# A hand-ordered attention and gate kernel: PSUM banks written into a table, and the compute tasks put in another order

## The chip, the cores and the metric

The kernel runs on one core of a Trainium2 chip. The metric is the device time of one execution in microseconds (us), as the median of several runs. PE is the matrix engine, DVE the vector engine, ACT the scalar engine, POOL the general engine, SP the engine that issues most transfers.

## The reference

Attention over 8 batches, 12 heads, 448 positions and 64 numbers a head, in which the sum below the fraction has one more term; then a gate with a circular convolution along the positions, between two dense layers (D is 768):

```python
scores = q @ k.transpose / 8                     # (8, 12, 448, 448)
m = max(scores); e = exp(scores - m)
x = (e / (sum(e) + exp(-m) + 1e-9)) @ v          # then heads side by side: (8, 448, 768)
x1, x2, x3 = split(x @ w_proj)                   # w_proj (768, 2304)
x2_conv = irfft(rfft(x2, axis=1) * rfft(filter, axis=0))
y = x1 * x2_conv * x3
out = y @ w_out                                  # (8, 448, 768), float32
```

Inputs and output are float32 in HBM; the matmuls run in bfloat16.

## The kernel before, in words

**Tasks.** Nothing is issued while the tensors are walked through. Each piece of work (four matmuls, one evacuation of PSUM, one transfer) is added to a plan with `plan.add` (line 83): the engine, what it needs and makes, the buffers that it takes and gives back, and a function that issues it. The plan then hands out the tasks. Each engine issues its tasks in the order of their numbers in `plan.ORDER` (line 455), a tuple with one number for each of 2033 tasks. `plan.FLIP` (line 456) lists the tasks that run on their other engine, ACT instead of DVE or the reverse. An engine works strictly in the order issued: a task that waits holds up all that stand behind it on that engine, and the wait itself is put in from what the task reads and writes.

**PSUM.** There are 8 banks. Scores ("sc", up to 3 at once) and attention outputs ("op", up to 2) take pairs of banks, everything else ("hy", up to 5) one bank. Which bank a task gets is chosen by `spots` (line 171) among those that the plan believes to be free at that moment, mostly the one that has been free longest. A matmul that writes into a bank waits for whatever last read that bank.

**Work.** `attention(i)`, i from 0 to 47, does one pair of heads. On PE: the scores S (lines 947 and 952, four matmuls of 64 rows for each of four tiles), the last 64 keys' part of e times v (ER, line 977), the rest of it (V, line 997). On ACT: the exponentials e and er (line 966). On DVE: the division, `norm` (lines 1010 to 1012, result xb). Results go to the transposed activations xT by a DMA transpose (line 1056). `dense(b)` does one batch of the gate: on DVE the folds that make xf (lines 1125 and 1134); on PE the projection x2, called PS (line 1175); its copy and a DMA transpose that SP issues (line 1188, in two halves); the spectrum Z on PE (line 1223) and its copy xs; the product with the filter's spectrum, t and yh, on DVE (lines 1241 and 1247); the inverse I on PE (line 1319) with its copy cr; cw, cv and the last product y on DVE (lines 1335, 1337, 1346, 1361). The gates G (line 1273) are six matmuls each; x1 is the copied one, and g is x1 times the other, on DVE (line 1288). The output O (line 1091, begun four matmuls early as O4) goes through the copy os into one of three buffers osb and is stored by SP (lines 1403, 1406, 1409). All copies out of PSUM stand in one helper, line 486 on ACT and line 488 on DVE. The buffers osb are taken in turn, so the copy of a fourth output tile waits until the store of the first has landed.

**Order of the whole.** The dense work of batch b runs between the attention tasks of later batches. Loads of q, k, v and their DMA transposes run far ahead on SP's queue; POOL casts what was loaded (lines 733 and 759) and issues v and the weights. At the start PE turns q and k itself for two batches (T, lines 621 to 642; copies qT and kT), the tables of the transform are built (rps at line 847; its copy fr, lines 854 and 855 on ACT), and the filter's spectrum is taken (uw on DVE, hrs). Where the plan expects PE to be idle at the start it puts filler matmuls (line 1566); 38 more (line 1574) run first of all.

Of the kernel before, what the change touches and what calls it, by code (L numbers as in the profile page):

```python
# [41 lines left out]
class Plan:  # L42
# [17 lines left out]
    FLIP = ()  # L60
    FETCH = (4.6, 256, 150)
# [14 lines left out]
    def __init__(self, rings):  # L76
        self.size = rings
        self.tasks = []
        self.banks = {}
        self.kept = []  # L80
        self.open = []

    def add(self, eng, cost, want, emit, need=(), make=(), take=(), give=(), dma=0.0, run=256, n=1, after=0.0, begun=(), late=0.0, turn=False, part=None, keep=False, port=False, mode=None, alt=None, mm=None):
        if alt:
            own = (eng, cost)
            (eng, cost), alt = (alt, own) if len(self.tasks) in self.FLIP else (own, alt)
            emit = lambda f=emit, e=eng: f(e)
        want = self.ORDER[len(self.tasks)] if self.ORDER else want + self.SHIFT.get(part, 0.0)
        self.tasks.append((want, len(self.tasks), eng, cost, emit, need, make, take, give, dma, after, run, n, begun, late, turn, keep, port or eng == "POOL" and not dma, mode or ("full" if eng == "PE" and not keep else None), alt, 2 * (mm or max(1, round(cost / 0.17)) if eng == "PE" and cost else 0)))

    def run(self):
# [79 lines left out]
        def spots(t):  # L171

            found, count = {}, {}
            for r, tok in t[7]:
                if r not in self.CAP or (r, tok) in self.banks:
                    continue
                count[r] = count.get(r, 0) + 1
                have = sum(1 for o in self.banks if o[0] == r and gone.get(o, 1e9) > now + 1e-9)
                if have + count[r] > self.CAP[r]:
                    return None  # L180
                busy = {i for got in found.values() for i in got}
                open_ = [i for i in range(self.NBANKS) if i not in busy and until[i] <= now + 1e-9]
                if r in self.PAIRS:
                    pairs = [(max(until[i], until[i + 1]), i) for i in open_ if i % 2 == 0 and i + 1 in open_]
                    if not pairs:
                        return None
                    i = min(pairs)[1]
                    found[(r, tok)] = (i, i + 1)
                else:
                    if not open_:  # L190
                        return None
                    found[(r, tok)] = (min(open_, key=lambda i: (self.MATE and i ^ 1 in open_, i < self.LOW, until[i], i)),)
            return found

        def ready(t):
            e = t[2]
            if not self.ORDER and t[10] > now + 1e-9:
                return False
            for k in t[5]:
                if made.get(k, 0):  # L200
                    return False
                at, by = when.get(k, (0.0, e))
                if at + (self.LAT[by] if by != e else 0.0) > now + 1e-9:
                    return False
            if e in queues and t[9]:
                out = sum(h[2][12] for h in queues[e]) + sum(x > now + 1e-9 for x in landed[e])
                if out + t[12] > self.OPEN:
                    return False
            if spots(t) is None:
                return False  # L210
            new = {}
            for r, tok in t[7]:
                if (r, tok) in holds or r in self.CAP:
                    continue
                h = held[r]
                i = len(h) + new.get(r, 0) - self.size[r]
                new[r] = new.get(r, 0) + 1
                if i >= 0 and gone.get((r, h[i]), 1e9) > now + 1e-9:
                    return False
            return True  # L220

        while any(queue.values()):
            moved = False
            for e in queue:
# [9 lines left out]
                for key, at in spots(t).items():  # L234
                    self.banks[key] = at
                    for j in at:
                        until[j] = 1e9
# [9 lines left out]
                if t[20]:  # L247
                    after, block, shift = self.FETCH
                    wait, cost = 0.0, end - now
                    edge = (fed - shift) // block * block + block + shift  # L250
                    while edge <= fed + t[20]:
                        at = now + cost * (edge - fed) / t[20] + wait
# [35 lines left out]
        for i, (_, t) in enumerate(order):  # L288
            if i in full:
                self.fill(*full[i])  # L290
            if t[16]:
                mine = {x for key in t[8] for x in self.banks.get(key, ())}
# [46 lines left out]
def kernel(  # L339
# [101 lines left out]
    def couple(c):  # L441
# [6 lines left out]
    plan = Plan(  # L448
        {
            "e": NE, "er": 2 * NER, "k0": 2, "q0": 2, "u": 1, "w": 1, "xf": 1,  # L450
            "x2": 1, "x2s": 1, "x2h": 1, "xs": 2, "t0": 2, "t1": 2, "yh": 1, "g": 1, "x1": 2, "cr": 2, "cw": 1, "cv": 2, "yT": 1, "yR": 1,
            "os": 3,
        }
    )
# [61 lines left out]
    def staged(b):  # L516
# [3 lines left out]
        for hp in range(NHP):  # L520
# [6 lines left out]
            for n, (name, x, at, size) in enumerate(parts):  # L527
# [29 lines left out]
                if alone:  # L557
                    add("ACT" if first else "SP", 0.52 if first else 0.5, -21.0 if first else want + 0.1 * n, load,
                        make=[("s" + name, g)], after=hold, dma=0.95 if name == "q" else 0.71, run=50)
                elif hp % 2 == 0:  # L560
                    need = [("cv", g - 6), ("cv", g - 5)] if name == "v" and c >= 3 else []
                    if name != "v" and c >= 4:
                        need = [("c" + w, c - 4) for w in "kq"]
                    add("POOL", 0.73, want + 0.1 * n, load, need=need, make=[(made, g), (made, g + 1)], after=hold, dma=1.05 if name == "q" else 1.0, run=45)
                if hp == 0 and name != "q":
                    add("SP", 2.6, want + (0.05 if name == "k" else SLOT[0] + 0.05) if b == 0 else want - RE1 + 0.1 * n,
                        lambda name=name: rests_load(name, b),
                        need=[("cr" + name, b - 1)] if b else (), make=[("r" + name, b)],
                        dma=1.25, run=22, begun=[("ir", b)], n=4)
# [1055 lines left out]
    with (  # L1625
# [6 lines left out]
        for b in range(n_batches):  # L1632
            W["yT", b], W["yR", b // 2] = y, yr
            stable(b)
            plan = Plan(plan.size)
# [9 lines left out]
    with tc.manual_schedule(engines={E.PE, E.Pool, E.DVE, E.Activation, E.SP}):  # L1645
        plan = main
# [31 lines left out]
```

## Time and profile before

| What | Value |
|---|---|
| runs | 373.08, 374.23, 373.16 us; median 373.16 |
| profiled execution, span | 370.8 us (the page gives no other time of that execution) |
| PE busy | 356.4 us, 96% |
| DVE busy | 274.8 us, 74% |
| ACT busy | 237.5 us, 64% |
| POOL busy | 127.6 us, 34% |
| clock granted to PE, 40 slices | 9 tenths or more in each |

The span runs from the first to the last recorded work; the runs' times are about 2.4 us longer than it. "Busy" of PE counts overlapping pipelined matmuls, so 96% doesn't mean that only 4% is left to win, nor that so much can be won. A wait shows in the timeline as a bracket at the row that waited, with the engine, the tile and the line that it waited for.

### The profile page before, as it was taken

Reading aid. Unit: us, or ns where it says so; the run is one execution under the profiler, and the core shown is the slowest. Engines: PE = TensorE matmul, PEld = TensorE weight load, DVE = VectorE, ACT = ScalarE, POOL = GpSimd, SP = SyncE. Lnnn points to the kernel's source line nnn. Section 1 sums busy time; section 2 is a strip of 40 time slices with the busy share of each in tenths; the row PEclk is TensorE's granted clock in tenths of the full one; section 3 lists DMA queues with packets and bytes.
Section 4 is the critical chain, followed back from the end, with each engine's and each line's share of the span. In section 5 each row is a group of like instructions: output and inputs, shape, how many; then the busy total and the mean of one; then the engine's idle time right before and its main releaser. Section 6 shows DMA issues by size and latency. Waiting matters only on the chain. (4 is left out here: it accounts for less than half of the span.)

```text
span 370.8 us, 10707 instructions
## 1 busy us (share of the span) xinstructions
PE 356.4 (96%) x4300; PEld 211.8 (57%) x4300; DVE 274.8 (74%) x674; ACT 237.5 (64%) x379; POOL 127.6 (34%) x278
## 2 busy tenths in 40 slices
PE   7989999999999979999999999999999999999995
PEld 7666675554555545565555646665565655555552
DVE  5468659982789726897579977689459898779970
ACT  4999876756767548567565657867776561334343
POOL 9984251444625274265537523313100100000000
PEclk9999999999999999999999999999999999999999
DMA  9999999988999999999998799995830074125035
GB/s 169 194 191 204 207 207 205 206 169 160 168 242 156 229 214 208 235 242 192 206 182 202 166 245 192 262 208 122 171 72 1 7 196 89 42 45 170 4 129 172
DMA packets 133958, 61.93 MB, mean 167 GB/s; under 512 B 105165, under 2 KB 130704, under 8 KB 133904
## 3 DMA queue, kind: packets, MB, share of 16 engines
q1 hardware_dynamic: 111552, 48.71, 61.6%
q0 software_dynamic: 22112, 12.26, 25.4%
q8 instruction: 34, 0.56, 0.6%
q10 hardware_dynamic: 240, 0.23, 0.2%
q14 instruction: 20, 0.16, 0.2%
HBM read 43.86 MB, written 11.01 MB: 148 GB/s over the span
## 5 line engine op out<-in xcount | busy, mean ns | idle before, releaser
L966 ACT ACTIVATE e<-psum 128x896 bf16<-128x896 f32 x144 | 126.6, 920 | 40.8 <-PE psum L947 37.3
L1273 PE MATMUL psum<-xT,wproj_bf 128*128 128x448 bf16 x576 | 121.7, 353 | 0.1
L1273 PEld LDWEIGHTS <-wproj_bf 128*128 128x128 bf16 x576 | 53.4, 98 | 47.7 <-issue 5.0
L1091 PE MATMUL psum<-wout_bf,yT 128*128 128x384 bf16 x288 | 54.7, 326 | 0.8 <-DVE g L1288 0.4
L1175 PE MATMUL psum<-xf,wproj_bf 128*128 128x452 bf16 x252 | 53.9, 357 | 0.0
L947 PE MATMUL psum<-qT,kT 64*64 64x448 bf16 x576 | 45.4, 359 | 2.5 <-DVE g L1288 0.7
L997 PEld LDWEIGHTS <-e 128*128 128x128 bf16 x1152 | 42.0, 98 | 9.6 <-issue 5.2
L997 PE MATMUL psum<-vn,e 128*128 128x65 bf16 x1152 | 46.8, 194 | 0.0
L733 POOL CAST nat<-nat 112x512 bf16<-112x512 f32 x36 | 25.4, 708 | 44.7 <-DMA nat<-in_q_dram 41.8
L1241 DVE TENSOR_TENSOR t<-xs,hrs 113x768 bf16<-113x768 bf16 (+1 forms) x64 | 36.4, 578 | 2.9 <-ACT xs L486 2.3
L1288 DVE TENSOR_TENSOR g<-x,psum 128x448 bf16<-128x448 bf16 x48 | 29.2, 616 | 12.1 <-PE psum L1273 10.9
L1091 PEld LDWEIGHTS <-yT 128*128 128x128 bf16 x288 | 26.6, 98 | 19.9 <-issue 1.8
L1175 PEld LDWEIGHTS <-wproj_bf 128*128 128x128 bf16 x252 | 23.2, 96 | 22.2 <-issue 1.1
L486 ACT CAST x<-psum 128x448 bf16<-128x448 f32 (+1 forms) x39 | 20.4, 529 | 22.6 <-PE psum L1273 14.5
L759 POOL CAST nat<-nat 128x384 bf16<-128x384 f32 x36 | 21.5, 598 | 32.2 <-DMA nat<-in_k_dram 31.9
L486 ACT COPY osb<-psum 128x384 f32<-128x384 f32 x39 | 18.2, 486 | 20.1 <-PE psum L1091 15.9
L486 ACT CAST xs<-psum 113x384 bf16<-113x384 f32 (+1 forms) x41 | 19.2, 482 | 15.1 <-PE psum L1223 14.1
L1012 DVE TENSOR_TENSOR xb<-psum,den 128x896 bf16<-128x896 f32 x24 | 26.2, 1091 | 0.8
L486 ACT CAST cr<-psum 128x452 bf16<-128x452 f32 x35 | 18.0, 539 | 11.5 <-PE psum L1319 11.0
L947 PEld LDWEIGHTS <-kT 64*64 64x64 bf16 x576 | 15.6, 105 | 17.1 <-issue 12.9
L966 ACT ACTIVATE er<-psum 128x896 bf16<-128x896 f32 x24 | 22.2, 926 | 4.3 <-PE psum L952 3.5
L987 POOL MEMSET sinks<- 1x1 bf16 x18 | 1.6, 91 | 65.6 <-PE psum L977 65.6
(143 smaller groups left out, 501.3 us busy)
## 6 DMA issues: line engine op xcount, KB each, us to landing
nat<-in_q_dram SPq DMA_DIRECT2D x37, 224.0 KB, 3.8
out_dram<-osb SPq DMA_DIRECT2D x21, 384.0 KB, 3.5
nat<-in_k_dram SPq DMA_DIRECT2D x38, 192.0 KB, 3.9
nat<-in_v_dram POOLq DMA_DIRECT2D x15, 192.0 KB, 6.3
wproj_bf<-in_moe_w_proj_dram POOLq DMA_DIRECT2D x2, 1152.0 KB, 18.1
out_dram<-osb SPq DMA_DIRECT2D x12, 192.0 KB, 2.7
ks<-in_v_dram POOLq DMA_DIRECT2D x9, 192.0 KB, 4.9
rests<-in_k_dram SPq DMA_DIRECT2D x32, 48.0 KB, 4.3
```

Source lines behind the costliest of these rows:

```text
L486: nc.scalar.copy(to, of)
L733: lambda hp=hp, qsrc=qsrc: nc.gpsimd.tensor_copy(qn[:, hp].rearrange("p j (u d) -> p u j d", u=2), qsrc.rearrange("p (u j d) -> p u j d", ...
L759: lambda hp=hp, sv=sv: nc.gpsimd.tensor_copy(kn[:, hp // 2, 3 * (hp % 2) + 1 : 3 * (hp % 2) + 4].rearrange("p j (u d) -> p u j d", u=2), sv),
L947: nc.tensor.matmul(sc[r, u, 0:S], kT[b % 2][c, hp // 2, 3 * turned + t, r], qT[b % 2][c, hp, :])
L966: nc.scalar.activation(to, of, AF.Exp, scale=SCALE)
L997: nc.tensor.matmul(out_bank(u)[:, n + 3 * turned, :], P["e"][1 + t][:, o : o + 128], vn[b % 2][:, hp, 4 * u + t, :], start=False, stop=tur ...
L1012: nc.vector.tensor_tensor(W["xb", b][:, hp // 2].rearrange("p s (u d) -> p u s d", u=2), op[:, :, :, 0:DH], rec[:].unsqueeze(3).to_broadca ...
L1091: nc.tensor.matmul(ops[:n, :DCH], y[:, dt, 0:n], wout_bf[:, dt, ch * DCH : (ch + 1) * DCH], start=(dt == 0), stop=(dt == NDT - 1),)
L1175: nc.tensor.matmul(pps, wproj_bf[:, kt, D + dt * 128 : D + (dt + 1) * 128], W["xf", b][:, :, kt, 0:FQ], start=(kt == 0), stop=(kt == NDT - 1),
L1241: nc.vector.tensor_tensor(t[:K], L["xs", par, ch][:K], h, op=ALU.mult)
L1273: nc.tensor.matmul(p[:, :S], wproj_bf[:, kt, 2 * part * D + dt * 128 : 2 * part * D + (dt + 1) * 128], xT()[:, kt, 0:S], start=(kt == 0), ...
L1288: nc.vector.tensor_tensor(g[:, dt, :], L["x1", dt], p[:, :S], op=ALU.mult)
```

## The change

Two things. First, `add` notes for each tenant of PSUM (655 of them) a bank from a new table `BANK`, in the order in which the tenants first appear, and `spots` then gives that bank or, if the plan believes it taken, lets the task wait. Second, `ORDER` and `FLIP` hold other numbers. The work of each task, its transfers, its sizes and the plan's costs are as before. Lines behind line 195 move by up to 12.

```diff
     FLIP = ()
+    BANK = ()
...
         self.open = []
+        self.mine = {}
...
             emit = lambda f=emit, e=eng: f(e)
+        for r, tok in take:
+            if r in self.CAP and self.BANK:
+                self.mine.setdefault((r, tok), self.BANK[len(self.mine)])
         want = self.ORDER[len(self.tasks)] if self.ORDER else want + self.SHIFT.get(part, 0.0)
...
                 open_ = [i for i in range(self.NBANKS) if i not in busy and until[i] <= now + 1e-9]
-                if r in self.PAIRS:
+                mine = self.mine.get((r, tok))
+                if mine is not None:
+                    at = (mine, mine + 1) if r in self.PAIRS else (mine,)
+                    if any(i not in open_ for i in at):
+                        return None
+                    found[(r, tok)] = at
+                elif r in self.PAIRS:
...
-    plan.ORDER = (9, 0, 6, 1370, 8, 10, 1, 5, 13, 18, 20, 11, 68, 120, 2, 14, 23, 3, 21, 19, ...
+    plan.ORDER = (10, 6, 2, 1369, 9, 11, 1, 4, 13, 18, 19, 7, 73, 110, 3, 12, 21, 0, 20, 16, ...
+    plan.BANK = (5, 7, 4, 1, 7, 6, 4, 5, 5, 7, 5, 4, 5, 0, 6, 5, 2, 1, 1, 5, ...
-    plan.FLIP = (30, 49, 71, 87, 94, 98, 376, 378, 380, 438, 464, 971, 975, 977, ...
+    plan.FLIP = (29, 44, 83, 86, 93, 94, 376, 382, 386, 388, 437, 438, 969, 973, ...
```

In the issued program SP's 183 tasks keep their order, and so do POOL's transfers among themselves. PE has 684 tasks in both, of which 464 stand at another place, the median one by 1 place and the farthest by 22. DVE has 577 tasks instead of 579, with 468 of them moved, by at most 64 places; ACT has 380 instead of 378, of which 60 came from DVE while 58 went there. Of 655 banks 241 are other ones. The matmuls are the same but for the fillers, 88 instead of 47.

The first place is ACT at the start of the program. The rows are the copies of turned q and k (qT, kT), the exponentials (e, er) and the copy of the transform's table (fr). Before:

```order
L486 COPY kT0_89<-psum_115 128x384 [waits PE_49]
L966 ACTIVATE e1_97<-psum_115 128x2x448 [waits PE_49]
L966 ACTIVATE e0_96<-psum_115 128x2x448
L854 CAST fr_84<-psum_115 113x452
L855 ACTIVATE fr_84<-psum_115 113x226 [waits Activation_49]
L966 ACTIVATE e2_98<-psum_115 128x2x448 [waits PE_49]
L966 ACTIVATE e3_99<-psum_115 128x2x448 [waits PE_49]
```

and now:

```order
L498 COPY qT0_91<-psum_115 128x448 [waits PE_49]
L866 CAST fr_84<-psum_115 113x452 [waits PE_49]
L867 ACTIVATE fr_84<-psum_115 113x226 [waits Activation_49]
L978 ACTIVATE e0_96<-psum_115 128x2x448 [waits PE_49]
L978 ACTIVATE e1_97<-psum_115 128x2x448 [waits PE_49]
L978 ACTIVATE e2_98<-psum_115 128x2x448 [waits DVE_49,PE_49]
```

The two rows of fr went from behind the second exponential to ahead of the first, and ACT copies qT instead of kT.

The second place is DVE while the output of batch 1 begins, between the attention of pair 18 and 19 (its division is the xb here) and that of pair 20. DMAHW in a wait means that a transfer, here a store out of an osb buffer, has to land first. Before:

```order
L1012 TENSOR_TENSOR xb_2575<-psum_115,den1_108 128x2x7x64 [waits DVE_49]
L1361 TENSOR_TENSOR yR_1599<-g_1906,cv_2483 128x2x64
L1288 TENSOR_TENSOR g_2600<-x1_2491,psum_115 128x448 [waits DVE_49]
L488 COPY osb_2606<-psum_115 128x384 [waits DMAHW4_49,PE_49]
L488 COPY osb_2592<-psum_115 128x384 [waits DMAHW7_49,PE_49,Activation_49]
L488 CAST x1_2667<-psum_115 128x448 [waits PE_49]
L488 CAST x1_2693<-psum_115 128x448 [waits DVE_49,PE_49,Activation_49]
```

and now:

```order
L1024 TENSOR_TENSOR xb_2618<-psum_115,den1_108 128x2x7x64 [waits DVE_49]
L1373 TENSOR_TENSOR yR_1606<-g_1948,cv_2540 128x2x64
L1373 TENSOR_TENSOR yR_1606<-g_1948,cv_2595 128x2x64
L1300 TENSOR_TENSOR g_2636<-x1_2597,psum_115 128x448 [waits DVE_49,Activation_49]
L500 CAST x1_2670<-psum_115 128x448 [waits PE_49,Activation_49]
L500 COPY osb_2683<-psum_115 128x384 [waits DMAHW4_49]
L500 CAST x1_2703<-psum_115 128x448 [waits DVE_49,PE_49,Activation_49]
```

One copy of x1 moved ahead of the copy that waits for a store, and the other osb copy is no longer on DVE; it is on ACT. On PE the two gate tasks whose results are these two x1 (twelve matmuls of line 1273) moved from behind ER of pair 20 (line 977) to ahead of it. ER of pair 20 takes banks 6 and 7 in both programs; before, these held the two osb copies' outputs, and now bank 6 holds that of the one copy left on DVE and bank 7 that of the first x1.

More of the change, by code (lines that the diff above doesn't have):

```diff
@@ new lines @@
+    plan.BANK = (5, 7, 4, 1, 7, 6, 4, 5, 5, 7, 5, 4, 5, 0, 6, 5, 2, 1, 1, 5, 4, 0, 4, 1, 6, 2, 2, 0, 4, 0, 6, 2, 0, 6, 6, 6, 2, 4, 2, 2, 6, 0, 4, 4, 4, 6, 0, 0, 0, 2, 4, 0, 6, 2, 6, 2, 2, 6, 2, 0, 6, 0, 0, 4, 6, 6, 4, 4, 2, 0, 2, 4, 6, 6, 0, 0, 2, 2, 4, 0, 6, 6, 6, 0, 0, 0, 0, 4, 0, 2, 4, 4, 4, 6, 2, 4, 4, 6, 6, 6, 0, 2, 6, 0, 0, 4, 6, 4, 4, 2, 2, 4, 6, 0, 4, 0, 4, 0, 2, 2, 6, 4, 6, 4, 4, 4, 0, 4, 6, 2, 2, 0, 0, 4, 2, 2, 0, 4, 2, 6, 4, 6, 6, 2, 4, 2, 4, 2, 6, 2, 0, 2, 6, 4, 6, 4, 0, 4, 2, 2, 4, 0, 2, 6, 2, 6, 0, 4, 2, 6, 0, 4, 2, 6, 0, 4, 0, 6, 4, 4, 4, 6, 6, 4, 2, 2, 0, 0, 6, 0, 4, 6, 4, 4, 2, 6, 0, 2, 2, 6, 0, 6, 0, 4, 4, 6, 6, 2, 0, 4, 6, 2, 0, 2, 6, 2, 2, 6, 0, 6, 5, 7, 1, 0, 5, 3, 1, 4, 3, 7, 4, 4, 6, 5, 0, 0, 2, 2, 1, 0, 4, 4, 1, 2, 2, 5, 3, 0, 4, 0, 4, 1, 3, 5, 2, 5, 3, 7, 2, 3, 1, 2, 4, 6, 7, 2, 3, 4, 2, 3, 3, 1, 6, 3, 0, 1, 2, 7, 3, 2, 1, 1, 0, 0, 7, 6, 7, 7, 6, 4, 3, 2, 2, 7, 6, 0, 4, 0, 3, 0, 3, 3, 3, 7, 5, 0, 1, 1, 2, 2, 2, 5, 4, 3, 7, 6, 7, 7, 1, 5, 0, 2, 7, 0, 6, 4, 0, 1, 2, 0, 0, 1, 7, 3, 3, 2, 4, 1, 4, 3, 1, 0, 2, 6, 3, 4, 5, 0, 1, 7, 6, 0, 6, 0, 7, 1, 5, 4, 6, 3, 0, 5, 1, 2, 0, 0, 0, 5, 3, 2, 3, 2, 4, 4, 6, 6, 0, 2, 3, 4, 5, 5, 5, 5, 4, 7, 3, 7, 7, 0, 0, 1, 3, 7, 1, 5, 2, 6, 0, 5, 6, 7, 1, 3, 7, 0, 1, 5, 3, 7, 3, 0, 5, 4, 6, 2, 1, 4, 7, 1, 0, 1, 2, 7, 6, 6, 3, 7, 4, 2, 1, 0, 1, 2, 5, 2, 0, 7, 3, 5, 3, 1, 2, 6, 6, 1, 7, 5, 6, 3, 0, 5, 3, 4, 0, 7, 6, 5, 5, 0, 4, 2, 5, 3, 7, 1, 6, 4, 6, 5, 4, 1, 0, 4, 0, 1, 7, 6, 5, 4, 1, 6, 4, 2, 0, 4, 0, 6, 2, 1, 4, 7, 1, 4, 7, 3, 4, 2, 7, 7, 1, 1, 5, 0, 5, 0, 4, 0, 4, 1, 2, 3, 7, 3, 1, 1, 5, 7, 4, 0, 2, 6, 7, 5, 5, 4, 2, 4, 1, 7, 7, 6, 7, 6, 0)
@@ new lines @@
+    plan.FLIP = (29, 44, 83, 86, 93, 94, 376, 382, 386, 388, 437, 438, 969, 973, 975, 979, 983, 1005, 1007, 1043, 1074, 1105, 1107, 1110, 1114, 1121, 1125, 1211, 1213, 1223, 1240, 1256, 1258, 1260, 1276, 1286, 1288, 1298, 1346, 1348, 1368, 1372, 1379, 1383, 1390, 1398, 1400, 1406, 1424, 1428, 1436, 1469, 1472, 1481, 1486, 1505, 1518, 1525, 1545, 1551, 1573, 1577, 1604, 1607, 1611, 1618, 1635, 1640, 1647, 1649, 1659, 1669, 1677, 1679, 1693, 1701, 1703, 1717, 1721, 1743, 1770, 1775, 1779, 1794, 1804, 1842, 1852, 1856, 1869, 1876, 1902, 1905, 1909, 1954, 1958, 1966, 1972)
```

3 lines of the change are left out of this document (1 added, 2 removed).

## The prediction

> **What bounds the kernel now.** I read the page's first two parts, then the stretches, then the list of what PE waited for, then the timeline at each wait.
>
> ```profile
> span 370.8 us, 10707 instructions
> PE 356.4 (96%) x4300; PEld 211.8 (57%) x4300; DVE 274.8 (74%) x674; ACT 237.5 (64%) x379; POOL 127.6 (34%) x278
> PEclk9999999999999999999999999999999999999999
> ...
> core 0: us, PE busy (x) PEld busy (x) DVE busy (x) ACT busy (x) POOL busy (x), PEclk, DMA share, GB/s
> 0.00:30.00 30.00, 25.59 (x513) 19.41 (x514) 18.20 (x52) 24.24 (x36) 27.38 (x68) 1.00 1.26 185
> 30.00:124.00 94.00, 91.81 (x1201) 55.11 (x1198) 72.41 (x177) 67.82 (x110) 38.29 (x79) 1.00 1.14 194
> 124.00:134.00 10.00, 7.47 (x67) 3.77 (x65) 4.74 (x11) 5.83 (x9) 4.06 (x9) 1.00 1.00 222
> 134.00:240.00 106.00, 105.64 (x1276) 61.04 (x1275) 80.08 (x185) 70.62 (x109) 50.01 (x105) 1.00 1.09 212
> 240.00:371.00 131.00, 125.93 (x1255) 72.48 (x1252) 99.34 (x251) 69.03 (x118) 7.92 (x20) 1.00 0.43 102
> ```
>
> PE sets the end: it streams matmuls nearly without a gap, so only its waits and its added work move the time. A stretch's length less PE's busy time gives them: 4.4 us before 30, 2.2 to 124, 2.5 in the ten us to 134, 0.4 to 240, 5.1 after, in which the last copy and store lie. DVE and ACT have room on average; they matter where PE waits for one of their tasks. The transfers' share is 1.0 or more until 240 and 0.43 after: until 240 a landing may be set by what the queues can move, not by when PE gets there. I return to that.
>
> ```profile
> PE psum L977 <- DVE osb L488: 2.5, 2, 2.3
> PE psum L1223 <- DMA x<-ldm: 0.8, 1, 0.8
> PE psum L1319 <- DVE x L488: 0.4, 1, 0.4
> ```
>
> (Total us, times, longest.) One wait stands out, 2.3 us. The others are places where a bank or an operand is still in an evacuation.
>
> **How a wait is sized.** Ends of matmuls are modelled, so I go from start to start:
>
> ```profile
> 62.98 0.37 PE L1319 MATMUL psum<-bt,yh 113*128 113x113 bf16 x4
> 63.76 0.37 PE L1319 MATMUL psum<-bt,yh 113*128 113x113 bf16 x4 [0.41 <-DVE x L488]
> 63.97 0.92 PE L997 MATMUL psum<-vn,e 128*128 128x65 bf16 x24
> ```
>
> Four such matmuls take 63.97 − 63.76 = 0.21 us; the second four start 0.78 after the first, so the wait cost 0.57, its bracket 0.41 plus 0.16. I add 0.16 to each bracket below.
>
> **The change, part by part.** *The long wait.*
>
> ```profile
> 124.72 0.41 SPq L1406 DMA_DIRECT2D out_dram<-osb  x1
> 131.66 1.02 DVE L488 COPY osb<-psum 128x384 f32<-128x384 f32 x2 [3.81 <-DMA out_dram<-osb]
> 132.27 0.19 PE L977 MATMUL psum<-vn,er 64*64 64x65 bf16 x1 [2.25 <-DVE osb L488]
> 132.73 0.29 PE L977 MATMUL psum<-vn,er 64*64 64x65 bf16 x13 [0.28 <-DVE osb L488]
> 334.14 1.30 PE L1273 MATMUL psum<-xT,wproj_bf 128*128 128x448 bf16 x6
> 335.27 0.33 PE L1223 MATMUL psum<-x,ft 113*112 113x384 bf16 x1
> ```
>
> A store issued at 124.72 lands before 131.66; only then may DVE copy two output tiles, and ER of pair 20 waits for both their banks (first bank 2.41, second 0.44 by the rule). In the new order twelve gate matmuls of line 1273 come ahead of ER; six take 335.27 − 334.14 = 1.13 us, twelve 2.26. The second copy is on ACT, so nothing but the first copy holds ER. If the store lands when it did, PE reaches ER with 2.26 more done and spends 0.44 less, 2.7 in all; counting matmuls up to ER in both orders (by their start-to-start times) gives another 0.37 of work moved ahead: 3.1 us. Queued behind the waiting copy on DVE are the second x1 and its g, whose gates now run early; if their bank were wanted first, they would be the next to be late. Only if PE gained time earlier and the store landed earlier too is more won here.
>
> *The waits before it.*
>
> ```profile
> 76.86 0.82 PE L1091 MATMUL psum<-wout_bf,yT 128*128 128x384 bf16 x4 [0.31 <-DVE yT L1361]
> 115.91 0.38 PE L947 MATMUL psum<-qT,kT 64*64 64x448 bf16 x4 [0.47 <-DVE g L1288]
> 95.21 1.84 SPq L1188 DMA_TRANSPOSE x<-ldm  x1
> 102.98 0.53 PE L1223 MATMUL psum<-x,ft 113*113 113x384 bf16 x2 [0.81 <-DMA x<-ldm]
> ```
>
> At 63.8 the copy that held the bank goes to ACT and the inverse gets another bank: −0.57. At 76.9 the last y is ahead of a fold on DVE: −0.47. At 115.9 that g moves ahead of cw on DVE: −0.63. The wait at 103 stays: its transpose, issued at 95.21, holds the same place on SP, and the spectrum needs it at the same point of PE's work.
>
> *The start.*
>
> ```profile
> 10.36 0.54 ACT L854 CAST fr<-psum 113x452 bf16<-113x452 f32 x1
> 10.93 0.36 ACT L855 ACTIVATE fr<-psum 113x226 bf16<-113x226 f32 x1
> 25.15 0.57 PE L947 MATMUL psum<-qT,kT 64*64 64x448 bf16 x8 [0.42 <-DVE xb L1012]
> 28.87 0.28 PE L977 MATMUL psum<-vn,er 64*64 64x65 bf16 x10 [0.74 <-issue]
> ```
>
> The 0.9 us of fr leaves the middle of the first exponentials, which PE's scores wait for there; but the xb awaited at 25.15 now has uw ahead of it on DVE, so that wait stays. The wait at 28.9 (0.9) should go, since no ACT copy stands between any longer. The 41 added fillers cost nothing where PE waits anyway; without that cover, 41 at 0.05 (the 113-column row above: 0.21 for four) are 2.1 us. I take −1.0 from the start: bounds −1.5 and +2.1, nearer the first, as 21 of the fillers stand right ahead of the scores of 25.15.
>
> So the start and 63.8, 76.9 bring −2.0 by 103. But the transpose at 103 and the store at 131.66 come out of queues that are full (share above 1.0). If they land when they did, those 2.0 and the 0.6 of 115.9 are waited away again, and the 3.1 at 132 is the whole gain until there. I take that: SP's order is unchanged, its transfers are issued back to back there, and PE's earlier arrival triggers none of those two.
>
> *After it.*
>
> ```profile
> 178.52 0.65 PE L1091 MATMUL psum<-wout_bf,yT 128*128 128x384 bf16 x3 [0.36 <-DVE g L1288]
> 259.33 0.38 PE L947 MATMUL psum<-qT,kT 64*64 64x448 bf16 x4 [0.25 <-DVE g L1288]
> 362.47 1.14 PE L1091 MATMUL psum<-wout_bf,yR 128*128 128x384 bf16 x6 [0.18 <-ACT osb L486]
> ```
>
> All three wait for a bank that the table changes: 0.52, 0.41 and 0.34, −1.3 together.
>
> *Costs.* PE passes between 64-row and 128-row matmuls 174 times instead of 168.
>
> ```profile
> 326.69 1.14 PE L1091 MATMUL psum<-wout_bf,yT 128*128 128x384 bf16 x6
> 327.66 1.33 PE L1175 MATMUL psum<-xf,wproj_bf 128*128 128x452 bf16 x6
> 299.49 0.49 PE L1091 MATMUL psum<-wout_bf,yT 128*128 128x384 bf16 x2
> 299.91 0.38 PE L952 MATMUL psum<-qT,kT 64*64 64x448 bf16 x4
> ```
>
> Six matmuls of line 1091 take 0.97, 0.162 each; two and the passage take 0.42, so a passage costs 0.10, six of them 0.6. Moving instructions among ACT and DVE (60 one way, 58 the other) is free while both have a quarter of their time idle.
>
> New waits: in batches 6 and 7 the first Z now follows the last PS that its transpose needs with less PE work between.
>
> ```profile
> DMA to landing us min/median/max: 3.6/4.2/7.7
> 327.45 7.01 SPq L1188 DMA_TRANSPOSE x<-nat  x2
> out_dram<-osb SPq DMA_DIRECT2D x21, 384.0 KB, 3.5
> ```
>
> Before, from the issue at 327.45 to the first Z of batch 7 (335.27, shown above) there were 7.8 us, and the transpose takes 3.6 to 7.7 (the row of the landings of line 1188). By the matmuls between in the new order there are 4.2. So 0 where it lands in 4.2 or less, up to 3.5 at the slow end; two more transposes (batch 6's first half, batch 7's second) have about 0.5 more room each. With transfers at 0.43 there, I take the quick end, and 0.3 for all three.
>
> Sum: −3.1 − 1.3 + 0.6 + 0.3 = −3.5 on a span of 370.8, so 367.3. The median of the runs, 373.16, stands 2.36 above the profiled span; the forecast is **369.7 us**.
>
> **A rule that speaks against it.** The granted clock is 9 tenths or more in all 40 slices and 1.00 in each of the five stretches, the one with the 2.3 us wait included. The Trainium skill, page "TensorE: Matmul & The Clock Gate", section "A second HAM failure mode: psum-queue depth-cycling", reports a kernel that cycles through PSUM banks every iteration with short idles of PE between groups, in which the clock went back and forth between half and full. A new bank table and new short waits could bring that about here. By the trace so far they don't: 8 banks are already cycled, with waits of 0.2 to 2.3 us. If it came, a stretch such as 124 to 134, with 7.5 us of PE work, would take 7.5 us more, and the time 377.
>
> **The rivals.**
> *The landings come earlier too.* For: buffers are freed sooner when the compute runs sooner, and then SP issues sooner. Against: the share above 1.0. It adds the 2.0 and 0.6: 367.1 us. Decided by whether the transfer awaited at 103 lands within 0.3 us of then.
> *New waits eat half.* 464 tasks of PE and 468 of DVE moved; the 2.2 us of waits from 30 to 124 were made by just such neighbours. If 2.0 come back at other places, behind 132, the time is 371.7.
> *The list is only another draw.* If the store's wait at 132 remains too (it lands later by as much as PE is kept busy, since it is issued behind others), nothing is gained: 373.2. For: that one landing took 6.9 us, when the median of such stores is 3.5 (the page's row above, after the transposes'), so it can swing by 3. Against: a swing is as likely to bring it earlier.
> *Slower: the last batches' transposes.* If those of line 1188 in batch 7 take the 7.7 us seen at worst, PE waits 3.5 for the first half and, as the second half's PS now stands behind that Z, about 3.0 for the second: 369.7 + 6.5 = 376.2. It decides from two landings of 6.8 each, where 4.6 us are lost. For: the cover shrank from 7.8 to 4.2. Against: the low share there.
>
> **How the numbers follow.** Forecast (368.6 to 370.8) 0.42; earlier landings (366.3 to 368.6) 0.22; half eaten (370.8 to 372.2) 0.12; another draw 0.11; slower through the transposes 0.11, through the clock 0.02. A difference under about 0.3%, 1.1 us, can't be told from none: faster means under 372.0, slower over 374.3. Faster 0.42 + 0.22 + 0.11 of the half-eaten = 0.75; same 0.12; slower 0.13. The range 366.4 to 373.3 leaves out the slower 0.13 and a part of the draw and of the fastest, under 0.2.
>
> **What would show it.** Right: no wait of PE at 132 over 0.7 us, and the store awaited there landing at 131 to 132; Z at 103 still waiting, longer than 0.8; no wait of the scores for g at 115.9 and of line 1091 at 178; PE's whole stream within 0.6 us of before. Wrong: a store landing at 128 (the gain is larger), brackets of over 1 us at Z with a DMA as releaser after 300 (smaller), a clock row with digits under 9, or a DVE bracket of several us ahead of a copy that PE waits for.

## The result, and the profile after

The change made the kernel slower: 376.54 us (median of 10 runs, 374.47 to 377.79) against 372.81 (10 runs, 371.81 to 374.72). The ratio is 1.0101, with a 95% interval of 1.0070 to 1.0133; forecast were 369.7 us and a range of 366.4 to 373.3. The profiled execution of the changed kernel took 374.84 us with a span of 373.1, so it lies 1.7 us under the median; the two spans are 2.3 us apart, so the traces show 2.3 of the 3.7 us between the medians.

The same views as before, the page first, then the stretches (columns as in the prediction: busy us of each engine, granted clock, transfers' share, GB/s):

```profile
span 373.1 us, 10784 instructions
PE 360.2 (97%) x4341; PEld 214.3 (57%) x4341; DVE 276.4 (74%) x672; ACT 239.6 (64%) x381; POOL 128.1 (34%) x278
PEclk9999999999999999999999999999999999999999
```

```profile
0.00:30.00 30.00, 27.46 (x519) 21.34 (x523) 18.38 (x51) 23.37 (x35) 25.07 (x66) 1.00 1.28 186
30.00:124.00 94.00, 91.67 (x1220) 55.94 (x1219) 72.56 (x176) 69.28 (x111) 38.65 (x82) 1.00 1.08 194
124.00:134.00 10.00, 9.62 (x73) 4.67 (x70) 6.60 (x15) 5.68 (x10) 4.65 (x9) 1.00 1.24 247
134.00:240.00 106.00, 103.83 (x1267) 59.56 (x1266) 80.79 (x181) 68.71 (x104) 49.28 (x101) 1.00 1.04 208
240.00:373.10 133.10, 127.67 (x1274) 72.83 (x1272) 98.07 (x252) 72.54 (x125) 10.50 (x23) 1.00 0.44 102
```

The hole of 2.5 us between 124 and 134 is closed (9.62 busy of 10). From 134 to 240, where PE had been idle for 0.36 us, it is now idle for 2.2. PE's list of waits has no long one any more, and more short ones:

```profile
PE psum L1235 <- DMA x<-ldm: 1.0, 1, 1.0
PE psum L1285 <- DVE ldm L500: 0.9, 1, 0.9
PE psum L1187 <- DVE xf L1146: 0.7, 1, 0.7
PE psum L959 <- DVE xb L1024: 0.6, 2, 0.4
PE psum L1103 <- ACT ldm L498: 0.4, 1, 0.4
PE psum L1235 <- DMA x<-nat: 0.4, 1, 0.4
```

A list of waits misses one kind here: fillers count as work. So I summed PE's waits over 0.15 us from start to start of the real matmuls, fillers left out, by stretch:

| Stretch, us | before | after |
|---|---|---|
| 0 to 55 | 7.16 | 9.02 |
| 55 to 150 | 5.77 | 3.13 |
| 150 to 262 | 1.12 | 3.37 |
| 262 to the end | 0.82 | 0.78 |

With 0.37 us of added passages between 64 and 128 rows (the matmuls at their own spacing take 345.7 us, not 345.4), that is +1.8 of the 2.3 us between the two spans. The rest lies behind PE: from the start of its last matmul to the end of the span it takes 5.2 us (367.87 to 373.05) instead of 4.6 (366.20 to 370.83). In this trace the middle gains 2.6 us, and the stretches around it lose more.

The start. On DVE the copy uw of the filter now stands ahead of the division (xb), and waits for its load. Before and after:

```profile
24.00 1.09 DVE L1012 TENSOR_TENSOR xb<-psum,den 128x896 bf16<-128x896 f32 x1
25.01 0.95 DVE L887 TENSOR_TENSOR uw<-filt 113x1536 bf16<-113x1536 bf16 x1
```

```profile
24.13 0.96 DVE L899 TENSOR_TENSOR uw<-filt 113x1536 bf16<-113x1536 bf16 x1 [3.17 <-DMA filt<-in_moe_filter_fft_dram]
25.48 1.09 DVE L1024 TENSOR_TENSOR xb<-psum,den 128x896 bf16<-128x896 f32 x1
```

```profile
24.60 0.38 PE L959 MATMUL psum<-qT,kT 64*64 64x448 bf16 x4
24.92 1.35 PE L1578 MATMUL psum<-idle 128*128 128x128 bf16 x21
26.62 0.57 PE L959 MATMUL psum<-qT,kT 64*64 64x448 bf16 x8 [0.36 <-DVE xb L1024]
```

The bracket says 0.36, but 21 fillers ran first: from 24.60 to 26.62 four scores were done, which take 0.19. The wait is 1.8 us, where it was 0.6.

Copies that wait for a landing stand out again behind 170 us: each holds a bank, and the work behind it on its engine. ACT at 177, then ACT and DVE at 217:

```profile
177.15 0.54 ACT L498 CAST ldm<-psum 128x452 bf16<-128x452 f32 x1 [1.81 <-DMA x<-ldm]
217.74 0.54 ACT L498 CAST ldm<-psum 128x452 bf16<-128x452 f32 x1 [3.48 <-PE psum L1187]
217.86 0.63 DVE L500 CAST ldm<-psum 128x452 bf16<-128x452 f32 x1 [1.94 <-PE psum L1187]
```

```profile
177.75 1.14 PE L1103 MATMUL psum<-wout_bf,yT 128*128 128x384 bf16 x6 [0.43 <-ACT ldm L498]
207.51 1.33 PE L1187 MATMUL psum<-xf,wproj_bf 128*128 128x452 bf16 x6 [0.17 <-DVE cr L500]
210.71 1.33 PE L1187 MATMUL psum<-xf,wproj_bf 128*128 128x452 bf16 x6 [0.28 <-ACT cr L498]
218.55 1.29 PE L1285 MATMUL psum<-xT,wproj_bf 128*128 128x448 bf16 x6 [0.89 <-DVE ldm L500]
```

At 177 the copy stands behind the same exponential as before, but a copy of x1 that stood ahead of it now stands behind, and its transpose landed at 177.08 instead of 175.20. The rows at 217.74 and 217.86 name PE, but by the modelled ends the twelve matmuls that they read (from 213.37, 2.50 us) were done at 215.87, and ACT and DVE begin within 0.12 us of each other: what they share is the buffer ldm, out of which the transpose of the first half, issued at 212.65, was read. That landing is missing from this trace, so the cause is inferred. The trace of clean_late (below), which holds the same two copies, has it: issued at 212.00, landed 3.8 us later, and ACT's copy began at once:

```profile
215.86 0.54 ACT L498 CAST ldm<-psum 128x452 bf16<-128x452 f32 x1 [2.25 <-PE psum L959]
```

In the kernel before, these copies stood on ACT behind the exponentials:

```profile
215.73 1.73 ACT L966 ACTIVATE e<-psum 128x896 bf16<-128x896 f32 x2 [1.79 <-PE psum L947]
217.34 1.43 ACT L486 CAST ldm<-psum 128x452 bf16<-128x452 f32 x3
```

### The profile page after: what moved, and what is told of

It reads as the page before. It is cut to its first block, busy times and chain, and to the rows that moved or that the text cites. A ratio compares the mean times of both kernels' runs of the same rounds, so it can differ in the third digit from the quotient of the medians.

```text
span 373.1 us, 10784 instructions
## 1 busy us (share of the span) xinstructions
PE 360.2 (97%) x4341; PEld 214.3 (57%) x4341; DVE 276.4 (74%) x672; ACT 239.6 (64%) x381; POOL 128.1 (34%) x278
## 5 line engine op out<-in xcount | busy, mean ns | idle before, releaser
L1187 PE MATMUL psum<-xf,wproj_bf 128*128 128x452 bf16 x252 | 54.9, 357 | 1.1 <-DVE xf L1146 0.7
L1103 PE MATMUL psum<-wout_bf,yT 128*128 128x384 bf16 x288 | 53.5, 326 | 0.7 <-ACT ldm L498 0.4
L498 ACT CAST x<-psum 128x448 bf16<-128x448 f32 (+1 forms) x43 | 22.6, 531 | 18.8 <-PE psum L1285 14.0
L498 ACT COPY osb<-psum 128x384 f32<-128x384 f32 x37 | 17.4, 482 | 20.4 <-PE psum L1103 13.0
L959 PEld LDWEIGHTS <-kT 64*64 64x64 bf16 x576 | 14.6, 105 | 20.0 <-issue 16.7
L1259 DVE TENSOR_TENSOR yh<-t 112x384 bf16<-112x384 bf16 (+1 forms) x64 | 24.1, 398 | 0.3
L498 ACT CAST cr<-psum 128x452 bf16<-128x452 f32 x32 | 16.5, 540 | 11.9 <-PE psum L1331 8.9
```

The lines of the kernel that those rows point to most:

```text
L498: nc.scalar.copy(to, of)
L959: nc.tensor.matmul(sc[r, u, 0:S], kT[b % 2][c, hp // 2, 3 * turned + t, r], qT[b % 2][c, hp, :])
L1103: nc.tensor.matmul(ops[:n, :DCH], y[:, dt, 0:n], wout_bf[:, dt, ch * DCH : (ch + 1) * DCH], start=(dt == 0), stop=(dt == NDT - 1),)
L1187: nc.tensor.matmul(pps, wproj_bf[:, kt, D + dt * 128 : D + (dt + 1) * 128], W["xf", b][:, :, kt, 0:FQ], start=(kt == 0), stop=(kt == NDT - 1),
L1259: nc.vector.tensor_tensor(yh[:K, par, n, ch * DCH : (ch + 1) * DCH], t[:K, 0, :], t[:K, 1, :], op=(ALU.subtract, ALU.add)[n],)
```

## The experiments

Each was timed beside the kernel before, in 6 or 12 runs; a ratio is to that, and 1.0101 is the changed kernel's. In brackets stand 95% intervals. In the runs that join two orders, a task takes order, flip and bank from the one or the other by its number.

**Which stretch.** Two halves first, cut at about 50 us:

```diff
+ORDER = before's for the tasks numbered under 340 there, the changed kernel's for the rest
+FLIP, BANK likewise            # start_before; start_only has the two exchanged
```

> Order, flips and banks of the changed kernel for the tasks up to about 50 us, those of before from there on. Theory A (what is lost at the start stays lost): ratio to before 1.003 to 1.004 (1.3 to 1.5 us). Theory B (PE meets transfers that land at times of their own at 103 and 143, so what is lost or won ahead of them is waited away): ratio 1.000.

> The other half: before's order, flips and banks up to about 50 us, the changed kernel's from there on. Theory A: ratio 1.0101 less 0.004, so about 1.006. Theory B: as the changed kernel, 1.009 to 1.010, all of the loss behind 150 us.

start_only: 1.0035 (1.0005 to 1.0065). start_before: 1.0089 (1.0055 to 1.0122). Both lose, and together, 1.24 per cent, they come to the whole within the intervals. start_only speaks for theory A, though its interval reaches almost down to none; start_before lies at theory B's 1.009, and its interval holds A's 1.006 as well. So the start's loss is likely real, and how much of it reaches the end is not settled.

Then the middle alone (tasks 340 to 900, about 60 to 155 us), and what stands around it:

```diff
+ORDER = before's under 340, the changed kernel's from 340 to 900, before's behind   # seg_mid
+ORDER = the changed kernel's under 900, before's behind                             # tail_before
+ORDER = before's under 900, the changed kernel's behind                             # tail_only
```

> Order, flips and banks of before, but for the tasks from about 60 to 155 us, which have those of the changed kernel. In that stretch the changed kernel made up 2.6 us against before. Theory A (waits add up): 372.8 - 2.6 = 370.2, ratio 0.993. Theory B (landings at 103 fixed): what is won before 103 is lost there, 1.9 remains, ratio 0.995. Rival: the gain isn't carried to the end, since later landings were as late, ratio 1.000.

seg_mid: 1.0004 (0.9974 to 1.0033): nothing is won. Its trace shows where a gain can go. Ahead of 103 PE was a microsecond earlier at the same place of its work than before, and at 132 it had no long wait. But:

```profile
103.49 0.70 PE L1235 MATMUL psum<-x,ft 113*113 113x384 bf16 x3 [2.29 <-DMA x<-ldm]
143.37 0.38 PE L959 MATMUL psum<-qT,kT 64*64 64x448 bf16 x4 [1.36 <-DMA qT<-nat]
157.42 0.38 PE L959 MATMUL psum<-qT,kT 64*64 64x448 bf16 x2 [0.20 <-DVE osb L500]
158.42 0.81 PE L1103 MATMUL psum<-wout_bf,yT 128*128 128x384 bf16 x4 [0.51 <-ACT osb L498]
```

The transpose at 103 landed at 103.45 here (102.94 before, 103.54 after; over the traces of the other runs from 102.0 to 105.1), and 1.5 us of the middle's lead are waited away at 143 for a q. The two waits at 157 and 158 belong to the cut, where the two orders hold different tasks; neither kernel has them. They cost 1.0 us by their rows, what was left of the lead at that point, so the middle without them would stand near 0.998: that its gain is lost to landings alone is not shown. In the changed kernel's own trace PE waited for no q at 143.

> The changed kernel up to about 155 us, before's order, flips and banks from there. Theory A: the start's loss of 0.0035 remains and the middle's gain of 2.6 us is kept, ratio 0.996 to 1.000. Theory B: the middle's gain is waited away at landings behind 155, in before's order too, ratio 1.003 to 1.004, the start's loss alone.

> Order, flips and banks of before up to about 155 us, the changed kernel's from there to the end. Theory A (the new order of 155 to 262 us waits by itself): the changed kernel's extra 2.2 us of waits there show, ratio 1.005 to 1.007. Theory B (PE waits there because the middle let it run ahead of the transfers): with before's middle PE comes a microsecond later to the same landings, ratio 1.000 to 1.002.

tail_before: 1.0047 (1.0016 to 1.0078), the same 1.0 us of the cut in it; without that it would lie near 1.002, between the two theories. tail_only: 1.0128 (1.0081 to 1.0175). By the ratio the changed order behind 155 us loses by itself, without any lead to run into the landings. But this cut, too, made waits of its own, 2.6 us:

```profile
156.13 0.32 PE L1235 MATMUL psum<-x,ft 113*113 113x384 bf16 x1 [1.28 <-DVE g L1300]
157.40 0.81 PE L1103 MATMUL psum<-wout_bf,yR 128*128 128x384 bf16 x4 [0.95 <-ACT osb L498]
```

Take them off, and about 0.6 per cent is left. A part of that is the clock: the mean granted clock of tail_only's runs is 0.994, that of the runs of before beside them 0.997, and at about 0.27 us for each thousandth (an estimate from two of tail_1's runs, at the end of this text) that is 0.8 us, 0.2 per cent. What is left can't be told from none by this run alone. The tail in two, cut at about 238 us:

> Before's order, flips and banks, but for the tasks from about 155 to 238 us, which have the changed kernel's. If the waits at 207 to 222 (banks and the copies behind a landing) make the tail's loss: ratio 1.006 to 1.010. If the loss lies behind 238: 1.000 to 1.002.

> The other part: before's up to about 238 us, the changed kernel's from there to the end. By the trace of the changed kernel, which wins 0.6 us there at 257 to 260 and 0.35 at the end and loses 0.46 at 310: ratio 0.998 to 1.000. If the loss lies here: 1.006 or more.

tail_1 (155 to 238): 1.0163 (1.0114 to 1.0212), with the same 2.6 us of the cut, 0.8 of the cut at 238 (a wait of PE at 246.03 that neither kernel has) and, at a mean granted clock of 0.993 against 0.998, by the same estimate 1.4 of the clock; of its 6.1 us some 1.3 are left. tail_2 (238 to the end): 0.9999 (0.9966 to 1.0032). So nothing is lost behind 238, and the stretch from 155 to 238 is found by exclusion more than by its own run. To be rid of the cut's waits I took two places where both orders have done the same tasks but for one, about 181 and 248 us; the second run moves three numbers back:

```diff
+ORDER = before's under 1066, the changed kernel's from 1066 to 1464, before's behind   # clean_late
-ORDER x2s(4,4) 1266, x2s(4,3) 1267 (on DVE); BANK G(4,0,1) 5
+ORDER x2s(4,3) 1274.3 (on ACT), x2s(4,4) 1274.6; BANK G(4,0,1) 6                      # clean_fixed, in addition
```

> Order, flips and banks of before, but for the tasks from about 181 to 248 us, which have the changed kernel's. Both cuts lie where the two orders have done the same tasks, so no wait comes from the cut itself (the cut at 155 of the earlier runs had its own, 1.1 to 2.6 us at 156 to 159). If the changed kernel's waits at 187, 207, 211, 218 and 220 (2.8 us in its trace) are the loss behind 155: ratio 1.006 to 1.0075. If the loss comes of the lead won in the middle, or of the places from 155 to 180: under 1.003.

> The same, with the two copies x2s(4,3) and x2s(4,4) behind the exponentials of pair 33 on ACT as before, and G(4,0,1) in bank 6. If the copies put ahead of other work while they wait for a landing are the half of that loss: 1.4 us less than clean_late, ratio 1.002 to 1.004. Rival (the wait moves on to the next bank): within 0.4 us of clean_late.

clean_late: 1.0076 (1.0042 to 1.0110). clean_fixed: 1.0033 (1.0001 to 1.0066). By the ratios they are 1.6 us apart, by the medians 0.5; the intervals overlap, so whether the two copies are half of this loss stays open. The cuts were not clean either. In both runs PE waits twice behind 248, as in clean_late:

```profile
252.10 0.37 PE L1331 MATMUL psum<-bt,yh 113*128 113x113 bf16 x4 [0.68 <-DVE g L1300]
259.69 0.50 PE L1103 MATMUL psum<-wout_bf,yT 128*128 128x384 bf16 x2 [0.78 <-DVE yT L1373]
```

By the rule of the brackets that is 1.8 us, where before waits 0.6 in the same stretch (257.6 and 259.3): 1.2 us in each trace come from the cut. And in clean_late's profiled execution the landing came early enough that the copies ran at 215.9 and PE didn't wait at 217 at all. If that wait makes a loss, it does so in some executions only.

**Single numbers.**

```diff
-ORDER uw(1) 121
+ORDER uw(1) 126.5      # uw_late: behind xb(2,3), which has 126
```

> The changed kernel, with one number of the order altered: on DVE the copy uw(1) of the filter stands behind the division of pairs 2 and 3 again, not ahead of it. Theory A (each wait of PE adds up to the end): the wait of the scores at 26.6 us falls from 1.84 to about 0.5, and the time by 1.3 against the changed kernel (376.5), to a ratio of about 1.0065 to before. Theory B (transfers that land at a fixed time swallow what is won or lost ahead of them): the wait at 26.6 goes, but the wait for the transpose at 103 grows by as much, and the ratio stays at 1.010.

uw_late: 1.0023 (0.9994 to 1.0052), median 374.76 us beside 373.16 of before. By the ratio one number of 2033 takes back most of the loss, by the medians a little over half (1.6 us are left of 3.7); either is more than the 1.3 us of its own wait. The trace does not bear it out as the work of this one place. The wait at the scores is 0.7 instead of 1.8, but other waits take it up: the 20th exponential on ACT starts at 26.4 instead of 27.3, but of the 2.0 us that the 36th is late, only 0.3 are won back (before, after, uw_late):

```profile
53.81 0.92 ACT L966 ACTIVATE e<-psum 128x896 bf16<-128x896 f32 x1 [0.39 <-PE psum L947]
55.76 0.92 ACT L978 ACTIVATE e<-psum 128x896 bf16<-128x896 f32 x1 [0.23 <-PE psum L959]
55.42 0.92 ACT L978 ACTIVATE e<-psum 128x896 bf16<-128x896 f32 x1 [0.23 <-PE psum L959]
```

The profiled execution, 371.19, is the fastest of the twelve, and no wait for the transpose came at 103 in it. The granted clock was high, too (mean 0.999 over its runs, 0.997 for before's beside them; by the estimate above 0.5 us). The loads of the filter were issued at the same 12.4 us as in the changed kernel and landed 9.1 to 10.0 us later instead of 10.4 to 11.3: landings move by a microsecond between executions. The reverse in the kernel before:

> The kernel before, with one number of its order altered: on DVE the copy uw(1) of the filter stands ahead of the division of pairs 2 and 3, as in the changed kernel. If this one place makes the start's loss: the wait of the scores at 25 us grows by 1.3 to 1.8 us, ratio 1.003 to 1.005. If later landings take it up, or if the start's loss has many causes: under 1.002.

uw_early_b: 1.0017 (0.9981 to 1.0052). The scores' waits grow from 0.6 to 1.2 us only, though the filter landed at 25.0 in its trace (22.4 before, 24.0 after), and the loss can't be told from none. So this one place is not shown to make the start's loss.

```diff
-ORDER count 6, identity 2
+ORDER count 2, identity 6      # count_first, on POOL
```

> The changed kernel with one swap on POOL: the count of rows and columns ahead of the identity, as before. DVE's four phase operations, 1.91 us beside POOL's fills in the changed kernel and 0.92 before, get back to about 0.92 if it is who comes first that decides; the first scores come 0.6 to 0.8 us earlier. The end: by waits that add up, 0.002 less than the changed kernel; if the exponentials' chain takes it up by 15 us, as the trace has it, no difference.

count_first: 1.0103 (1.0052 to 1.0154). The phases do go back to 0.93 us (below), and the end doesn't move.

```diff
-BANK of G(4,0,1): 5
+BANK of G(4,0,1): 6      # g_bank
-plan.BANK = (...)         # no_bank, from the changed kernel too
```

> The changed kernel, with one number of the bank table altered: the gate task G(4,0,1) gets bank 6, as before, not bank 5, which a copy of x2 holds that stands on DVE behind a transfer. Theory A (this one bank makes the wait at 218.6): 1.07 us of PE's wait goes and the time falls by about 1.0, to a ratio of 1.007. Rival: the copy itself is late, and DVE and ACT with it, so the wait turns up again within the next few tasks; under 0.3 us is won, ratio 1.010.

> The changed kernel without its bank table: banks are chosen by the planner as before, the order and the list of flips are the new ones. If the order makes the difference: a ratio of 1.006 to 1.013, with other small waits. If the bank table does: the waits that name a bank (at 76 to 78, 130, 178, 207, 211 and 218) go and the ratio falls to 1.000 or under.

g_bank: 1.0117 (1.0081 to 1.0152). The rival holds; the wait turns up at the next task, behind ACT's exponential:

```profile
220.86 0.32 PE L1235 MATMUL psum<-x,ft 113*112 113x384 bf16 x1 [1.87 <-ACT e L978]
```

So it isn't this bank that is late but the engines behind it. no_bank: 1.0090 (1.0056 to 1.0124): the loss is the order's, not the table's of banks. Moving the copies in the changed kernel itself:

> The changed kernel, but two copies of batch 4's projection, x2s(4,3) and x2s(4,4), that wait for the landing of the first half's transpose, stand on ACT behind the exponentials of pair 33 as before, instead of on DVE and ahead of them, and G(4,0,1) has bank 6. Theory (a wait for a landing was put ahead of DVE's and ACT's other work): PE's 2 us of waits from 207 to 222 fall under 1, ratio 1.005 to 1.006. Rival: PE is as late for the landings anyway, ratio 1.010.

> The changed kernel with three local repairs: uw(1) behind the division of pairs 2 and 3, POOL's count of rows ahead of the identity, and the two copies of the run x2s_late. If the loss lies in these places: ratio 0.998 to 1.001, with the long wait at 132 gone. If it is spread over many small places: still over 1.002.

x2s_late: 1.0113 (1.0075 to 1.0150). Its trace has 1.05 us of waits from 150 to 262 instead of 3.4, yet the runs' time is no better: a miss. Its profiled execution, 373.3, is the fastest of its six. repaired, all three: 1.0075 (1.0048 to 1.0103), far from the forecast of 0.998 to 1.001. It contains uw_late's change, and the two intervals barely touch; in its trace the 36th exponential starts at 57.0, later than in the changed kernel. So no run confirms that these places hold the loss; the result is the one forecast for a loss that is spread over many small places.

**Fewer bytes.**

```diff
-nc.sync.dma_start(out[b, st * 128 : (st + 1) * 128, :], osb)
+nc.sync.dma_start(out[b, st * 128 : st * 128 + 1, :], osb[0:1])      # batches 0 to 4
```

> The kernel before, with the stores of batches 0 to 4 cut to one row of each tile (some 6 MB of 62 left out; those rows of the output aren't written). If landings set the time up to 240 us: 1 to 3 us less, ratio 0.992 to 0.997, the wait at 132 among it. If PE's own order sets it but for that one wait: 2.4 us less at most, and nothing at 103 and behind.

> The changed kernel with the same stores cut. Theory B: with less on the queues its waits between 155 and 262 shrink from 3.4 to about 1.5 us and it loses its distance to before: the same ratio as less_store_b, within 0.003. Theory A: those waits stay, and the distance of 0.01 between the two remains.

less_store_b: 1.0017 (0.9983 to 1.0052); less_store_a: 1.0120 (1.0070 to 1.0170). Neither gets faster, and the distance stays. The long wait at 132 is gone in less_store_b and its time is the same: PE comes there a microsecond later than before, after a wait of 1.4 us at 104, and what it wins is given back at 195, in a wait of 1.2 us for a copy on DVE. That these bytes, 6.6 MB of 61.9 by the two profiles, make the landings late is out; the landing at 103 comes before the first store (109.8) in any case.

## Why the prediction was wrong, point by point

- **Where forecast and trace part.** The forecast span was 367.3 us, the trace's is 373.1. The sum had the start at nothing (its −1.0 was to be waited away at 103), and it cost 1.9. It had −3.1 up to 150, all of it at 132; the trace has −2.6 there. Behind 150 it had −1.0 (−1.3 for three banks, +0.3 of new waits), and the trace has +2.2. The passages were put at 0.6 and came to 0.4, and the last store's 0.5 wasn't in it. So two terms failed: most of all what lies behind 150, and next the start.
- **The long wait at 132: right.** ER ran at 134.23 without a bracket, behind the two gates, and the copy that waits for the store at 133.20, without a bracket either:

```profile
134.23 0.31 PE L989 MATMUL psum<-vn,er 64*64 64x65 bf16 x14
133.20 0.55 DVE L500 COPY osb<-psum 128x384 f32<-128x384 f32 x1
```

  From the last wait ahead of it PE gained 2.2 us on before there; 3.1 were forecast.
- **The wait at 103: right.** It stayed and grew:

```profile
103.59 0.70 PE L1235 MATMUL psum<-x,ft 113*113 113x384 bf16 x3 [0.99 <-DMA x<-ldm]
```

- **"I take −1.0 from the start", then at nothing in the sum: a step that failed.** By its own working the bounds were −1.5 and +2.1, and the trace came to +1.9 (9.02 against 7.16 us of waits to 55 us). The prediction saw uw ahead of the division and took the wait at 25.15 as unchanged, with the landing of 22.4 of the one trace. DVE was held to 24.1. The lead that fr's move gave, 0.24 us at the fifth exponential (12.54 against 12.78), was gone by the sixth (14.03 against 13.79). start_only puts the loss at 0.35 per cent; uw is not shown to be more than a part of it (uw_late, uw_early_b).
- **"If they land when they did, those 2.0 and the 0.6 are waited away": right in kind, but used only for what stands ahead of 132.** The sum counted 3.1 us at 132 as kept to the end. In seg_mid the middle's gain isn't kept: PE waits 2.4 us at 103, where before waits 1.0, and 1.5 at 143, both for landings, and 1.0 at the cut. In the changed kernel's own trace the gain stands until 150 us, and what follows costs 2.2. The prediction asked about a landing only ahead of 132, though the transfers' share is 1.09 until 240.
- **"All three wait for a bank that the table changes": one of three wrong.** The waits at 259 and 362 are gone. At 178 the new bank is held by a copy that waits for a landing: 0.59 us instead of 0.52. The prediction named the bank's new holder nowhere. In g_bank another bank only moved such a wait to the next task.
- **New waits, 0.3: the step that failed most.** They were looked for in the batches 6 and 7 only, which cost 0.5 (one wait at 310.38). The stretch from 150 to 262 has 3.4 us of waits, all but a few tenths from 177 to 222; the sum had none there. no_bank (1.0090) puts the loss on the order, not on the table of banks; which of its places make it stays open, since x2s_late, g_bank and repaired, which moved single ones, did not take it back. "New waits eat half" had the kind, a price of 2.0 and a chance of 0.12.
- **The rival on the other side was the wrong one.** Batch 7's first transpose took 3.8 us (the second has no landing in the trace), and PE waited for neither.
- **The clock: right to keep small.** It was granted at 1.00 in every stretch. Its mean over the runs of each kernel is 0.997 for both; single runs go down to 0.992 after and 0.988 before. By the rule of the Trainium skill, page "TensorE: Matmul & The Clock Gate", section "A second HAM failure mode: psum-queue depth-cycling", other banks and more short waits might have set it swinging; the runs show no difference.
- **The time around the span** is 1.74 us, by the list of runs (374.84 less 373.1); the 2.36 of the prediction mixed one execution's span with other runs' median. That made the forecast 0.6 us too high, so it hid a part of the miss: by luck, the error ran towards the result.
- **The table** of banks has 535 numbers, one for each tenant; the 655 of the part on the change counts both banks of the pairs.

What stays open: how the loss divides over the places of the start and those behind 155 us, and how much of what uw_late gives back is its own. The runs of one kernel spread over 3 to 8 us; the landings move by a microsecond or two between executions, the clock has a part in it, and one trace shows one draw of that. None of the 18 kernels is faster than the kernel before by more than the runs can tell.

## What to carry to other kernels

In a queue that runs strictly in order, look at what stands behind each operation that waits for a transfer: a place that costs nothing in one trace may cost when the landing slips by a microsecond. Putting such an operation later is worth trying, but these runs don't show that it pays: uw_late got faster, x2s_late did not, and repaired, which contains both, hardly. A lead won ahead of a landing may be waited away there; follow it to the next landing before it goes into the sum. Where an order changes at hundreds of places, price the whole stretch, not only the waits that the old trace shows. And cut and rejoin two orders only where both have done the same work, or the cut makes waits that neither has.

## What the hardware showed that I had not expected

DVE's four phase operations at the start (line 794 before, 806 after) took 0.92 us before and 1.91 after, the same instructions on the same sizes. What differs is who was first. After, POOL's fills of e began at 1.63 and DVE at 1.90:

```profile
1.90 1.91 DVE L806 TENSOR_SCALAR ph<-ci,row 128x113 f32<-128x113 int32 x4
```

```profile
1.63 0.20 POOL L1595 MEMSET e<- 128x128 bf16 x1
1.77 0.14 POOL L1596 MEMSET e<- 128x64 bf16 x1
2.94 0.14 POOL L1596 MEMSET e<- 128x64 bf16 x1
```

Before, DVE began at 1.47 and the fills at 1.71. Then DVE went at its own pace, and the fills took up to 2.8 times as long:

```profile
1.47 0.92 DVE L794 TENSOR_SCALAR ph<-ci,row 128x113 f32<-128x113 int32 x4
```

```profile
1.71 0.27 POOL L1583 MEMSET e<- 128x128 bf16 x1
1.92 0.22 POOL L1584 MEMSET e<- 128x64 bf16 x1
3.00 0.39 POOL L1584 MEMSET e<- 128x64 bf16 x1
```

In count_first, where POOL's count is first again, DVE has its pace back:

```profile
1.47 0.93 DVE L806 TENSOR_SCALAR ph<-ci,row 128x113 f32<-128x113 int32 x4
```

So the two engines slow each other there, and 0.43 us of a later start of DVE goes with which of them pays; with the next operations the sines came 1.8 us later (5.78 instead of 4.00). Why, the traces don't show.

The second: over all runs the mean granted clock of one execution lies anywhere from 0.984 to 1.000, and the time goes with it. Of tail_1's six executions the one with 0.999 has a span of 375.1 us, the one with 0.984 of 379.1, and the others lie between in both. A part of each kernel's spread is the clock, not the landings; between the kernels before and after it makes no difference, since both means are 0.997.
